# VectorE's share of the exponentials computed from two parts instead of three, with 232 units instead of 200

## The chip, the cores and the metric

The kernel runs on one core of a Trainium2 chip: TensorE (PE) multiplies matrices, ScalarE (ACT) evaluates functions, VectorE (DVE) does elementwise work, GpSimd (POOL) does little here but issue accumulating DMAs, and SyncE (SP) issues the other DMAs. Each engine works through its own instructions in order. TensorE writes its results to eight PSUM banks of 128 x 512 fp32, and ScalarE and VectorE read them there. The metric is the time of one execution on the device in microseconds; where several executions were timed, their median.

## The reference

Two attention branches read the same x (2048 x 640) and are mixed by a gate. The first is full softmax attention with 32 heads of 20 dimensions, the second looks at 8 keys with a step of 2 positions.

```python
qkv = (x @ wqkv).reshape(B, S, 3, H, Dh)             # H = 32, Dh = 20, S = 2048, D = 640
# branch A
scores = jnp.einsum("bhqd,bhkd->bhqk", q, k) * scale
p = _softmax(scores, axis=-1)
a = jnp.einsum("bhqk,bhkd->bhqd", p, v) ... @ wo
# branch B: keys at position s - 2*w, w = 0..7, own weights
logits = jnp.einsum("bhsd,bhswd->bhsw", q, kg) * scale   # masked below 0
b = jnp.einsum("bhsw,bhswd->bhsd", softmax(logits), vg) ... @ wo
g = sigmoid((x * gate_w).sum(-1, keepdims=True))
return g * a + (1 - g) * b
```

Branch A needs 32 x 2048 x 2048 exponentials. That is 134 million, or 1.05 million per partition.

## The kernel before

Branch A is cut into 32 groups: 4 blocks of 512 queries times 8 quads of 4 heads. A group has 64 units; a unit is one head, 128 keys and 512 queries, so 128 x 512 scores in one PSUM bank, and there are 2048 units. For each unit TensorE multiplies keys and queries (L1318), an exponential turns the scores into weights in SBUF, and TensorE multiplies these with the values into one PSUM bank for the group (L1425). The four heads of a quad use four strips of 32 rows or columns of TensorE, so up to four such matmuls run at the same time. A column of ones beside the values gives the softmax's sum, and the maximum over the keys enters the query projection as a bound (`KM`, L717), so no pass for the maximum is needed.

The exponential of most units is done by ScalarE (`mk_exp`, L1376), two or three banks in one instruction, in turn from banks 0 to 2 and from banks 3 and 4. Bank 5 is added as a third one where it is free. The other units go to VectorE, through bank 5 or 7. For them VectorE makes the exponential out of bits. The scores are scaled so that adding a constant and converting to int16 (L1584, one unit) gives the bit pattern of a bf16 number t: the integer part becomes the exponent E and the fraction the mantissa m, so t = E times m with m from 1 to 2. That is 2 to a power, with the curve between two powers replaced by a straight line. The rest mends the curve, two units at a time. `xw` takes the mantissa bits (L1614) and `xe` the exponent bits (L1618, with one low mantissa bit set, `XMU`); m is squared (L1622) and multiplied with t (L1625), which gives E times m cubed. TensorE then adds three parts for each unit: t with the values, `xe` with the values, and `xw` with the values scaled by `XCUB` = 0.168 (`vP`, made by GpSimd at L1391 for each change of the quad, 28 times, and kept in two buffers). The sum is E (1.008 + m + 0.168 m^3), and the constant `XKAP` in `XB` brings it to the scale of ScalarE's exponentials. A buffer of t (there are three) is free again when the third of its users has been issued.

The order of all instructions is fixed when the program is built. A planner (`_Sched`, the lanes and the loop at the end of `_build`) keeps a clock for each engine with written costs and places work step by step; one step is one exponential of ScalarE with the score matmuls ahead of it. Lanes hold the other work: key, query and value projections (`gen_k`, `gen_q`, `gen_v`), the normalisation of a group (`gen_norm`), the local branch (`gen_F` for its projections and score products, `gen_V` for its values, `gen_K` for its softmax and its products with the values), the output projection (`gen_fold`) and VectorE's units (`gen_xm` for the scores, `gen_xr` for the conversion, `gen_x` for the rest). Projections take one of banks 5 and 7, as VectorE's units do. The table `SEG` holds twenty settings of the planner for each stretch of 24 steps. Where TensorE has room and its share of work in the last microseconds is under the first of these, a spare matmul fills it (`spare`, L1946 to L1961); some of these add zeros to a bank that is in use, with the zero tile `zt` as weights and the identity as the moving side (L1951).

`gen_K` multiplies weights and values of the local branch in VectorE (L1149, L1159) into product buffers `tmps`, and accumulating DMAs from GpSimd's queue (L1161) add these into `accs`. For want of space these lie on other tensors: the first two accumulators are `accW`, whose second half also holds the key weights `WkP`; the second product buffer is block 0 of `xT`, and the other accumulators are block 1. So `gen_K` waits until all key projections, the query projections of block 0 and all value projections are done.

## Time and profile before

| | |
|---|---|
| median of 3 runs | 874.95 us (871.74 to 876.6) |
| profiled execution | 872.27 us, its span 870.5 us |
| TensorE busy | 788.9 us (91%) |
| VectorE busy | 746.8 us (86%) |
| ScalarE busy | 853.4 us (98%) |
| GpSimd busy | 127.4 us (15%) |
| TensorE's granted clock | 1.00 throughout |

A row of the group view names the line, the engine, the operation, what it writes and reads with shapes and the count, then the busy time, the mean duration of one in ns, and the idle time of the engine just ahead of these instructions with what ended it. Durations of neighbouring instructions overlap, so that the sum of single durations is more than the busy time. A row of the waits names who waited for whom, the total in us, how often, and the longest. A row of the table by stretches gives its length, the busy time of PE, PEld (weight loads), DVE, ACT and POOL with their instructions, the clock, and the DMA's share and rate.

### The profile page before, as it was taken

The page shows a single profiled execution, that of the slowest core. Times are in us where ns is not written, and L with a number is a line of the kernel's source. Part 1 is how long each engine was busy: PE and PEld are TensorE (multiplying, and loading weights), DVE is VectorE, ACT ScalarE, POOL GpSimd, SP SyncE. Part 2 cuts the span into 40 slices and gives each one's busy share as a digit, 9 for nine tenths or more (in the row PEclk, how much of TensorE's full clock was granted, in tenths as well). Part 3 has the DMA queues.
Part 4 walks back from the last instruction along what each step waited for, and adds up shares of the span by engine and source line. Part 5 has one row for each costly group of instructions (what it writes and reads, how often), then busy time and mean ns, then how long its engine had stood idle before and what let it go on. Part 6 is the DMA issues. An engine that isn't in the chain of part 4 may idle for free.

```text
span 870.5 us, 16946 instructions
## 1 busy us (share of the span) xinstructions
PE 788.9 (91%) x6951; PEld 250.6 (29%) x7039; DVE 746.8 (86%) x1322; ACT 853.4 (98%) x793; POOL 127.4 (15%) x131
## 2 busy tenths in 40 slices
PE   9989998999998999988998889988899998888997
PEld 6322332223223222222232223322222222222234
DVE  6587977888877878988998989999999989999985
ACT  6999999999999999999999999999999999999997
POOL 1100010000100112223132220332300001243000
PEclk9999999999999999999999999999999999999999
DMA  8222001010010135456557662485810014585001
GB/s 184 43 50 51 6 17 13 5 28 6 6 16 8 38 55 94 66 97 107 103 107 108 97 100 32 92 134 99 127 10 6 9 17 77 89 134 92 1 2 32
DMA packets 141313, 51.33 MB, mean 59 GB/s; under 512 B 120628, under 2 KB 128948, under 8 KB 141236
## 3 DMA queue, kind: packets, MB, share of 16 engines
q0 software_dynamic: 13824, 31.46, 21.3%
q1 hardware_dynamic: 126612, 18.59, 13.8%
q8 instruction: 56, 0.92, 0.4%
q10 hardware_dynamic: 800, 0.18, 0.1%
q14 instruction: 21, 0.17, 0.1%
HBM read 16.14 MB, written 2.62 MB: 22 GB/s over the span
## 4 chain that ended last, share of the span: by engine, by line
ACT 80%; DVE 10%; PE 5%; DMA 4%; issue 1%; POOL 0%; DVEq 0%
ACT ebuf L1376 79%; DMA xT<-xT 2%; DMA accW<-tmps 1%; PE ps L1318 1%; DVE xT L1159 1%; DVE xt L1584 1%; DVE prod L1019 1%; DVE tmps L1159 1%; PE ps L506 1%; PE ps L1204 1%; DVE xw L1625 1%; DVE xw L1622 1%; PE ps L1228 1%; PE ps L1425 1%; DVE xe L1618 1%
## 5 line engine op out<-in xcount | busy, mean ns | idle before, releaser
L1376 ACT ACTIVATE ebuf<-ps 128x1536 bf16<-128x1536 f32 (+1 forms) x767 | 839.8, 1396 | 3.7 <-PE ps L1318 3.3
L1318 PE MATMUL ps<-qT,kT 32*128 32x512 bf16 x1984 | 296.6, 384 | 59.8 <-ACT ebuf L1376 45.9
L1425 PE MATMUL ps<-ebuf,vA 128*21 128x512 bf16 (+2 forms) x1964 | 216.4, 369 | 1.0 <-DVE rg L764 0.7
L1584 DVE TENSOR_SCALAR xt<-ps 128x512 int16<-128x512 f32 x200 | 136.1, 685 | 45.3 <-PE ps L1318 43.1
L1318 PEld LDWEIGHTS ps<-qT,kT 32*128 32x128 bf16 x1984 | 72.7, 91 | 326.7 <-ACT ebuf L1376 279.5
L1391 POOL TENSOR_SCALAR vP<-vA 128x1344 bf16<-128x1344 bf16 x28 | 39.1, 1397 | 423.3 <-DVE vA L635 241.2
L1625 DVE TENSOR_TENSOR xw<-xt,xw 128x1024 bf16<-128x1024 bf16 x100 | 69.5, 695 | 1.6
L1622 DVE TENSOR_TENSOR xw<-xw 128x1024 f16<-128x1024 bf16 x100 | 68.4, 684 | 0.0
L1425 PEld LDWEIGHTS ps<-ebuf,vA 128*21 128x21 bf16 x1964 | 45.3, 90 | 60.7 <-issue 49.6
L1425 PE MATMUL ps<-xw,vP 128*21 128x512 bf16 (+2 forms) x212 | 58.1, 372 | 0.0
L506 PE MATMUL ps<-xT,WqkB 128*128 128x512 bf16 x175 | 53.7, 383 | 4.1 <-issue 2.5
L1425 PE MATMUL ps<-xe,vA 128*21 128x512 bf16 (+2 forms) x212 | 56.4, 373 | 0.0
L1614 DVE TENSOR_SCALAR xw<-xt 128x1024 uint16<-128x1024 uint16 x100 | 43.6, 436 | 13.5 <-PE ps L1425 12.8
L1019 DVE TENSOR_TENSOR prod<-qk 128x1024 bf16<-128x1024 bf16 x80 | 52.6, 688 | 0.2
L1161 POOL DMA_DIRECT2D accW<-tmps x36 | 32.2, 971 | 129.7 <-DVE tmps L1159 93.3
L1425 PE MATMUL ps<-xt,vA 128*21 128x512 bf16 (+2 forms) x212 | 48.7, 373 | 0.2 <-DVE rg L764 0.2
L506 PE MATMUL ps<-xT,WqP 128*128 128x512 bf16 x138 | 42.8, 383 | 2.2 <-issue 2.0
L1618 DVE TENSOR_SCALAR xe<-xt 128x1024 uint16<-128x1024 uint16 x100 | 44.5, 445 | 0.0
L506 PE MATMUL ps<-xT,accW 128*128 128x512 bf16 x125 | 38.3, 383 | 1.8 <-issue 1.1
L1951 PE MATMUL ps<-ident,zt 128*128 128x512 bf16 x106 | 34.9, 385 | 0.3 <-issue 0.3
L506 PE MATMUL ps<-WvA,oBacc 128*128 128x320 bf16 x160 | 31.2, 302 | 1.2 <-DVE qT L720 0.9
L720 DVE TENSOR_SCALAR qT<-ps 128x512 bf16<-128x512 f32 x32 | 22.0, 688 | 11.1 <-PE ps L717 5.3
(134 smaller groups left out, 801.2 us busy)
## 6 DMA issues: line engine op xcount, KB each, us to landing
accW<-tmps POOLq DMA_DIRECT2D x36, 320.0 KB, 4.2
accW<-xT POOLq DMA_DIRECT2D x24, 320.0 KB, 4.1
xT<-xT POOLq DMA_DIRECT2D x24, 320.0 KB, 4.2
WqkB<-in_B_wqkv_dram SPq DMA_DIRECT2D x40, 160.0 KB
xT<-tmps POOLq DMA_DIRECT2D x12, 320.0 KB, 4.6
WqP<-in_A_wqkv_dram SPq DMA_DIRECT2D x135, 20.0 KB
x_tm<-in_A_x_dram SPq DMA_DIRECT2D x8, 320.0 KB
out_dram<-outsb SPq DMA_DIRECT2D x24, 80.0 KB
```

The costliest lines, as they stand in the source:

```text
L506: ins = e.matmul(o, l, r, start=(k0 + k == 0), stop=(k0 + k == n - 1))
L1019: t = T("dve", lambda e, r=r, q_ap=q_ap, k_ap=k_ap: e.tensor_tensor(prod[r][:, :, :], q_ap, k_ap, ALU.mult), reads=["qB", "kB"], writes=[( ...
L1318: return e.matmul(o, kT[js, q, kb * P:(kb + 1) * P], qT[g % NQT][js, :], start=True, stop=True)
L1376: return T("act", lambda e: e.activation(ebuf[:, 512 * p:512 * (p + n)], ps[:, b0 * 512:(b0 + n) * 512], ACTF.Exp, scale=LN2 / ONE), reads ...
L1391: T("pool", lambda e, r=r, q=q: e.tensor_scalar(vP[r % NVP][:, :, :], vA[:, q, :, :], XCUB, 1.0, op0=ALU.mult, op1=ALU.mult), reads=[("vA" ...
L1425: ins = e.matmul(bank[OB][32 * j:32 * j + DH + 1, o:o + w], vv, ap[:, w * i:w * i + w], start=st and i == 0, stop=sp and i == len(ks) - 1)
L1584: r = T("dve", lambda e, b=b, i=i, sl=sl: e.tensor_scalar(xt[sl][:, 512 * i:512 * i + 512].bitcast(I16), bank[b], XB, 0.0, op0=ALU.add, op ...
L1614: T("dve", lambda e, r=r, t0=t0: e.tensor_scalar(xw[r][:, :].bitcast(U16), t0.bitcast(U16), 0x007F, 0x3F80, op0=ALU.bitwise_and, op1=ALU.b ...
L1618: tx = T("dve", lambda e, r=r, t0=t0: e.tensor_scalar(xe[r][:, :].bitcast(U16), t0.bitcast(U16), 0x7F80, XMU, op0=ALU.bitwise_and, op1=ALU ...
L1622: T("dve", lambda e, r=r: e.tensor_tensor(xw[r][:, :].bitcast(F16), xw[r][:, :], xw[r][:, :], ALU.mult), reads=[], writes=[("xw", r)], cos ...
L1625: t = T("dve", lambda e, r=r, t0=t0: e.tensor_tensor(xw[r][:, :], t0, xw[r][:, :].bitcast(F16), ALU.mult), reads=tk, writes=[("xw", r)], c ...
L1951: T("pe", lambda e: e.matmul(bank[OB], zt[:, :], ones4, start=False, stop=False, skip_group_check=True), reads=["ident", "zt"], accum=[("o ...
```

## The change

VectorE's units use two parts in place of three. The mantissa bits are now combined with the exponent of one half, so `xw` holds m/2, and one multiplication with t gives E times m^2 / 2; there is no square. TensorE adds `xe` with the values and `xw` with the values, so E (1.016 + m^2 / 2). The part with t itself, GpSimd's scaled values `vP` and the code that planned them go, and a buffer of t is free as soon as the product has been issued. `XKAP` and `XMU` have new values.

The number of VectorE's units comes out at 232 instead of 200, and most rows of `SEG` are new, so all work is placed anew. In the built programs ScalarE's exponentials are 306 of three units and 449 of two, where they were 314 and 453.

Space has moved too. The key weights `WkP` have a tile of their own. `zt` has two columns in place of 128; the first matmuls of the program, which used it, take 128 zeroed columns of `oTd`. The zero spares take the identity as weights and, as the moving side, the two columns of `zt` read 256 times (`zrow`). For the first block, `gen_K` no longer waits for the projections (`dead0`); until these are done it uses only the first product buffer.

```diff
-XKAP = 2.174928977877578
+XKAP = 1.512810100254
 XB = 127.0 * ONE - ONE * float(np.log2(XKAP))
-XMU = 0x0001
-XCUB = 0.16796875
+XMU = 0x0002
...
 SEG = {
-    0: (0.68, -1e9, 20, 20, 0, 8, 380000.0, 1, 500.0, 0, 0.6, 40, 20, 600.0, 14000.0, 3, 6, 4, -1, 30.0),
+    0: (0.68, 300.0, 34, 12, 60, 10, 360000.0, 0, 0.0, 0, 0.6, 60, 20, 3000.0, 14000.0, 3, 6, 4, -1, 30.0),
...
-    zt = sb([P, P], BF16, "zt")
+    zt = sb([P, 2], BF16, "zt")
+    zrow = fap(zt, zt[:, 0:1], [[0, 256], [1, 2]])
...
-    WkPt = accW[:, 2 * D:4 * D]
+    WkPt = sb([P, 2 * D], BF16, "WkP")
...
-    NVP = 2
-    vP = [sb([P, KBN, 4 * VW], BF16, "vP%d" % i) for i in range(NVP)]
...
+    T("dve", lambda e: e.memset(oTd[:, 0, 0:P], 0.0), writes=["zw"])
...
+    def dead0():
+        return bool(fdone.get(0) and vBdone.get(0)) and all(i in kl and kl[i].done and GI[(0, i)] in ql and ql[GI[(0, i)]].done
+                                                           for i in range(1, NQUAD)) and all(i in vl and vl[i].done for i in range(4))
+
     def gen_K(tc):
...
-        while not (all(i in kl and kl[i].done and GI[(0, i)] in ql and ql[GI[(0, i)]].done for i in range(1, NQUAD)) and all(i in vl and vl[i].done for i in range(4))):
+        while tc > 0 and not dead0():
             yield ("poll",)
...
-                m = tmctr[0] % NTM
+                m = tmctr[0] % NTM if tc > 0 or dead0() else 0
...
-    def vp_make(r):
-        q = GO[QL[r]][1]
-        vpdone.add(r)
-        T("pool", lambda e, r=r, q=q: e.tensor_scalar(vP[r % NVP][:, :, :], vA[:, q, :, :], XCUB, 1.0, op0=ALU.mult, op1=ALU.mult),
-          reads=[("vA", q, g) for g in range(6)], writes=[("vP", r % NVP)], cost=1600)
...
-                    vv = vA[:, q, kb, VW * j:VW * j + DH + 1] if part < 2 else vP[QW[min(g, HG)] % NVP][:, kb, VW * j:VW * j + DH + 1]
+                    vv = vA[:, q, kb, VW * j:VW * j + DH + 1]
...
-                xleft[ids[i]] = 3
-                xpend.append((("xt", sl, i), xt[sl][:, 512 * i:512 * i + 512], un, 0, g, r, ids[i], ("t", sl)))
+                xleft[ids[i]] = 2
...
-            T("dve", lambda e, r=r, t0=t0: e.tensor_scalar(xw[r][:, :].bitcast(U16), t0.bitcast(U16), 0x007F, 0x3F80, op0=ALU.bitwise_and, op1=ALU.bitwise_or),
-              reads=tk, writes=[("xw", r)], cost=XTS)
-            yield ("dve", XTS, 0.0)
             xbusy[r] = 4
             tx = T("dve", lambda e, r=r, t0=t0: e.tensor_scalar(xe[r][:, :].bitcast(U16), t0.bitcast(U16), 0x7F80, XMU, op0=ALU.bitwise_and,
                                                                 op1=ALU.bitwise_or),
                    reads=tk, writes=[("xe", r)], cost=XTS)
+            yield ("dve", XTS, 0.0)
+            T("dve", lambda e, r=r, t0=t0: e.tensor_scalar(xw[r][:, :].bitcast(U16), t0.bitcast(U16), 0x007F, 0x3F00, op0=ALU.bitwise_and,
+                                                           op1=ALU.bitwise_or),
+              reads=tk, writes=[("xw", r)], cost=XTS)
             yield ("dve", 690.0, 0.0)
-            T("dve", lambda e, r=r: e.tensor_tensor(xw[r][:, :].bitcast(F16), xw[r][:, :], xw[r][:, :], ALU.mult),
-              reads=[], writes=[("xw", r)], cost=690)
-            yield ("dve", 690.0, 0.0)
-            t = T("dve", lambda e, r=r, t0=t0: e.tensor_tensor(xw[r][:, :], t0, xw[r][:, :].bitcast(F16), ALU.mult),
+            t = T("dve", lambda e, r=r, t0=t0: e.tensor_tensor(xw[r][:, :], t0, xw[r][:, :], ALU.mult),
                   reads=tk, writes=[("xw", r)], cost=690)
             xcred[0] -= 1
-            xput_t(sl)
+            xfree.append(sl)
...
-            T("pe", lambda e: e.matmul(bank[OB], zt[:, :], ones4, start=False, stop=False, skip_group_check=True),
+            T("pe", lambda e: e.matmul(bank[OB], ident[:, :], zrow, start=False, stop=False, skip_group_check=True),
```

## The prediction

> **What bounds the kernel now.** I read the profile's page first: the engine totals and the 40 slices.

> ```profile
> span 870.5 us, 16946 instructions
> PE 788.9 (91%) x6951; PEld 250.6 (29%) x7039; DVE 746.8 (86%) x1322; ACT 853.4 (98%) x793; POOL 127.4 (15%) x131
> DVE  6587977888877878988998989999999989999985
> ACT  6999999999999999999999999999999999999997
> PEclk9999999999999999999999999999999999999999
> L1376 ACT ACTIVATE ebuf<-ps 128x1536 bf16<-128x1536 f32 (+1 forms) x767 | 839.8, 1396 | 3.7 <-PE ps L1318 3.3
> ```

> ScalarE is busy in 98% of the span, and 839.8 us of that is one line, the 767 exponentials of L1376. Before them it idled 3.7 us in all. VectorE is next, and full in the second half. Then the table by stretches, to see whether this holds everywhere, and the start and the end:

> ```profile
> core 0: us, PE busy (x) PEld busy (x) DVE busy (x) ACT busy (x) POOL busy (x), PEclk, DMA share, GB/s
> 120.00:150.00 30.00, 27.19 (x209) 7.53 (x210) 23.48 (x38) 29.19 (x28) 2.97 (x2) 1.00 0.13 21
> 450.00:480.00 30.00, 27.07 (x264) 8.79 (x264) 26.79 (x39) 29.57 (x29) 9.77 (x11) 1.00 0.71 115
> 600.00:630.00 30.00, 24.56 (x218) 6.76 (x220) 27.60 (x45) 29.57 (x28) 10.47 (x12) 1.00 0.88 145
> 750.00:780.00 30.00, 25.96 (x231) 7.09 (x231) 28.79 (x42) 30.00 (x28) 11.38 (x12) 1.00 0.70 115
> 780.00:810.00 30.00, 26.69 (x241) 7.24 (x241) 29.51 (x50) 30.00 (x28) 7.56 (x8) 1.00 0.49 87
> 18.64 12.75 ACT L1376 ACTIVATE ebuf<-ps 128x1536 bf16<-128x1536 f32 x11 [0.80 <-PE ps L1318]
> 866.82 0.44 ACT L923 ACTIVATE WvB<-ps 128x320 bf16<-128x320 f32 x1 [2.34 <-PE ps L865]
> ```

> Even where VectorE is fullest (29.51 of 30 us at 780 to 810) ScalarE has 30.00: VectorE's work runs beside the exponentials. The waits and the chain say who waits for whom:

> ```profile
> PEld ps L1318 <- ACT ebuf L1376: 279.5, 587, 1.0
> ACT ebuf L1376 <- PE ps L1318: 3.3, 9, 0.8
> ACT 80%; DVE 10%; PE 5%; DMA 4%; issue 1%; POOL 0%; DVEq 0%
> ```

> TensorE's score matmuls wait for ScalarE to free their banks 587 times, and the other way round only 9 times, 3.3 us. So a microsecond of exponentials taken from ScalarE is a microsecond of time, as long as scores still come early. The chain's 10% on VectorE are short pieces of the local branch and the query projections in the middle; there the slack is thin.

> **The change part by part.** Units are 128x512 blocks of scores; there are 2048. In the built programs ScalarE has 314 exponentials of three units and 453 of two before, 306 and 449 after: 1848 units become 1816, VectorE's 200 become 232.

> ```profile
> L1376 ACT ACTIVATE ebuf<-ps 128x1536 bf16<-128x1536 f32 x314 | 516.4, 1645 | 1.8 <-PE ps L1318 1.5
> L1376 ACT ACTIVATE ebuf<-ps 128x1024 bf16<-128x1024 f32 x453 | 510.2, 1223 | 1.9 <-PE ps L1318 1.8
> ```

> *ScalarE.* The two forms differ by 1645 - 1223 = 422 ns, one unit. Records overlap (516.4 + 510.2 is more than 839.8), so the fixed part is what is left of the busy time: (839.8 - 1848 x 0.422) / 767 = 0.078 us. Removed: 32 x 0.422 + 12 x 0.078 = **14.4 us**. This is the gain, all of it on the path.

> *VectorE.* Each pair of units loses its square, and there are 16 more pairs.

> ```profile
> L1584 DVE TENSOR_SCALAR xt<-ps 128x512 int16<-128x512 f32 x200 | 136.1, 685 | 45.3 <-PE ps L1318 43.1
> L1625 DVE TENSOR_TENSOR xw<-xt,xw 128x1024 bf16<-128x1024 bf16 x100 | 69.5, 695 | 1.6
> L1622 DVE TENSOR_TENSOR xw<-xw 128x1024 f16<-128x1024 bf16 x100 | 68.4, 684 | 0.0
> L1618 DVE TENSOR_SCALAR xe<-xt 128x1024 uint16<-128x1024 uint16 x100 | 44.5, 445 | 0.0
> L1614 DVE TENSOR_SCALAR xw<-xt 128x1024 uint16<-128x1024 uint16 x100 | 43.6, 436 | 13.5 <-PE ps L1425 12.8
> ```

> Removed 100 x 0.684 = 68.4 us; added 32 x 0.685 + 16 x (0.695 + 0.445 + 0.436) = 47.1 us; net -21.3 us. The product now takes two bf16 operands instead of bf16 and f16; I price it at the same 695 ns, since L1622, with two bf16 operands, is at 684. VectorE lies beside ScalarE, so this by itself is worth nothing: it pays for keeping up with a path that is 14.4 us shorter. It does not help evenly. Counted in the programs' order, VectorE has 71 units beside exponentials 553 to 744 before and 86 after: 15 x 0.685 + 7.5 x 1.576 = +22.1 us against 35.5 x 0.684 = -24.3 us. There VectorE's work falls by 2.2 us while ScalarE's falls by 15 x 0.422 = 6.3 us. VectorE was full there, so up to 4.1 us of the gain can be given back; ScalarE lost nothing at 29.51 of 30 us, so I take 1.5.

> *TensorE.* The parts per unit go from three to two:

> ```profile
> L1425 PE MATMUL ps<-ebuf,vA 128*21 128x512 bf16 x1792 | 209.0, 382 | 0.9 <-DVE rg L764 0.7
> L1425 PE MATMUL ps<-xw,vP 128*21 128x512 bf16 x192 | 56.5, 385 | 0.0
> L1951 PE MATMUL ps<-ident,zt 128*128 128x512 bf16 x106 | 34.9, 385 | 0.3 <-issue 0.3
> ```

> 2368 value matmuls of 512 columns (1792 + 3 x 192) become 1762 + 2 x 222 = 2206, at 209.0 / 1792 = 0.117 us some 19 us less. TensorE waits for ScalarE 279.5 us, so the cover is large and this is worth nothing. The spare matmuls with zeros (106 plus 3 before, 82 after) now have the identity as weights and a two-element row of zeros read 256 times as the moving side. No row shows such an operand; by L1951's shape I take the same duration, and keep the rest for a rival.

> *GpSimd.* The 28 scaled copies go:

> ```profile
> L1391 POOL TENSOR_SCALAR vP<-vA 128x1344 bf16<-128x1344 bf16 x28 | 39.1, 1397 | 423.3 <-DVE vA L635 241.2
> L1614 DVE TENSOR_SCALAR xw<-xt x100: 359/419/1532, 54.5 to 851.2; 128x1024 uint16<-128x1024 uint16 x100
> POOL vP L1391 <- PE ps L1425: 146.4, 11, 26.5
> accW<-tmps POOLq DMA_DIRECT2D x36, 320.0 KB, 4.2
> ```

> L1614's longest is 1532 ns against a median of 419, about one vP (1397) longer. Mean less median, over 100 of each, is (436 - 419) x 100 = 1.7 us, off the path. [...] The accumulating DMAs queued behind a waiting vP (up to 26.5 us) on GpSimd's queue also start freely; they land in 4.2 us as before.

> *Local branch sooner.* The first accumulating DMA stands behind the 276th exponential before and the 268th after; until the other buffer is free only one product buffer is used, so each product waits for the last one's landing (4.2 us). The counts of products, DMAs and queue entries are unchanged, SP's too. Nothing else waits on this branch until its fold, some 100 exponentials on; cost 0, and at best it lifts part of the 3.3 us that exponentials wait. Bounds -3.3 to +1.

> *Placement.* Of 32 query projections, those finished three exponentials or fewer ahead of their first score number five before and two after (the first of all in both). The last value group of head quads 6 and 7 now stands directly ahead of the value matmuls that need it; before it was two exponentials ahead. TensorE then waits for its evacuation, with the next scores behind it:

> ```profile
> L635 DVE CAST vA<-ps x23: 285/657/659, 20.0 to 287.7; 128x480 bf16<-128x480 f32 x19, 128x160 bf16<-128x160 f32 x4
> L712 DVE TENSOR_SCALAR qabs<-ps 128x512 uint16<-128x512 uint16 x32 | 21.9, 684 | 8.9 <-PE ps L506 8.8
> L720 DVE TENSOR_SCALAR qT<-ps 128x512 bf16<-128x512 f32 x32 | 22.0, 688 | 11.1 <-PE ps L717 5.3 <-PE ps L1318 4.5 <-PE ps L617 0.8
> L717 PE MATMUL ps<-qabs,KM x21: 379/389/390, 57.7 to 822.3; 128*128 128x512 bf16 x21
> ```

> That is 0.3 us for the short form (the shortest of L635), at most one queued VectorE operation of 0.7 us more: 0 to 1.0 us, I take 0.5.

> *Start and end.* One more memset, of the 128 zero columns, ahead of TensorE's first matmuls; these end before x arrives. The first score and the tail keep their instructions. Both 0.

> **The sum.** The profiled execution took 872.27 us (span 870.5 and 1.8 around it): 872.27 - 14.4 + 1.5 + 0.5 = **859.9 us**. The median of the runs, 874.95, lies 2.7 above that execution, the fastest run, 871.74, just below it; I state 860. The low end takes away all 3.3 us of waits as well and adds none: 872.27 - 14.4 - 3.3 = 854.6. The high end has the 4.1 us, the 1.0 us and two late queries of 0.684 + 0.389 + 0.688 = 1.76 us each, 866.5, and the 2.7 us of the median: 869.

> **The rivals.**

> *VectorE takes over as the bound.* For it: its slices are at 9 from the middle on, and the chain is already 10% there. If in those 10% a shorter exponential stream gains nothing, and the 4.1 us come on top, the gain is 14.4 x 0.9 - 4.1 = 8.9 us: 863. Against it: 30.00 of ScalarE beside 29.51 of VectorE. Still faster.

> *Late queries: slower.* Two score banks serve both VectorE's units and every projection, and 32 more units hold them. If query projections are pushed out until scores wait for the whole chain of 1.76 us, the point from which the gain is gone is 14.4 / 1.76 = 8 of the 32; all 32 would give 872.3 - 14.4 + 56 = 914. Against it: only two of 32 stand so close in the order, and the present five cost at most 0.8 us each.

> *The change does not give what the counts say, through slow zero rows.*

> ```profile
> 17.16 0.59 PE L1291 MATMUL ps<-xT,ident 128*128 128x512 bf16 x2
> ```

> Two such matmuls in a row take 0.59 us, one takes 0.385, so one streams in 0.205. If the repeated two-element row streams at half rate, 82 x 0.205 = 16.8 us if all stood in the way of scores: 877. It decides from 12.4 / 82 = 0.15 us each on the path. Against it: spares are placed where TensorE has nothing to do, with 279.5 us of waiting as cover.

> *The clock.* TensorE has some 19 us less work. If the granted clock fell to half in one stretch of 30 us, its 27 us of work would need 54: about 24 us, 884. Against it: the stretch at 600 had 24.56 us of TensorE work at 1.00. [...]

> **How the numbers follow.** About 0.5%, 4.4 us, is what a measurement here can tell from no change. Forecast 0.72; VectorE as the bound 0.14; late queries 0.06; zero rows 0.04; clock 0.02; several small waits that just eat the gain 0.02. Faster: 0.72 + 0.14, and 0.02 of the late queries, 0.88. Same: 0.01 of the late queries, 0.02 of the zero rows, the 0.02 of small waits, 0.05. Slower: the rest, 0.07. The range 854.6 to 869 holds the first two cases and leaves out some 0.15 with their own tails.

> **What would show it.** 755 exponentials at the same 1645 and 1223 ns, L1376's line near 825 us, idle before it below 8 us; VectorE near 725 us busy; GpSimd near 88 us; no vP rows; the clock at 1.00. It is wrong if exponentials wait for scores more than 10 us, if the zero spares last longer than 385 ns, or if ScalarE's share falls below 97%.

## The result and the profile after

The changed kernel takes 864.14 us in the median of 4 executions (862.73 to 867.12), the kernel before 874.52 (871.74 to 876.60). The ratio is 0.9888, with a 95% interval of 0.9847 to 0.9929: faster by 1.1%. The forecast was 860 us; the median lies 4 us above it, inside the range. The profiled execution of the changed kernel took 865.48 us.

The lines of its page that answer to those shown of before (engine totals, slices of VectorE and of the clock, the group of the exponentials, the shares of the chain):

```profile
span 863.7 us, 16606 instructions
PE 798.3 (92%) x6862; PEld 246.9 (29%) x6862; DVE 716.9 (83%) x1303; ACT 839.3 (97%) x781; POOL 87.3 (10%) x103
DVE  6586867878777779888888998998699898999885
PEclk9999999999999999999999999999699999999999
L1377 ACT ACTIVATE ebuf<-ps 128x1536 bf16<-128x1536 f32 (+1 forms) x755 | 826.3, 1412 | 11.3 <-PE ps L1319 11.3
ACT 84%; DMA 6%; PE 5%; DVE 3%; issue 1%; POOL 0%; SPq 0%; DVEq 0%
```

The exponentials' busy time went from 839.8 to 826.3 us, 13.5 us less, but the idle time ahead of them rose from 3.7 to 11.3 us, and one slice of the clock is no longer full. The span fell by 6.8 us: 13.5 less 7.6, and 0.9 elsewhere. So the work left ScalarE as forecast, and what has to be explained is 7.6 us of waiting, where the prediction's sum had set aside 2.0. Two of the prediction's own signs of being wrong came up: the exponentials waited more than 10 us, and the zero spares last 391 ns, more than the 385 it allowed.

The table by stretches shows where it is (us, busy time of each engine, then clock, DMA share and GB/s):

```profile
core 0: us, PE busy (x) PEld busy (x) DVE busy (x) ACT busy (x) POOL busy (x), PEclk, DMA share, GB/s
600.00:630.00 30.00, 26.59 (x183) 5.62 (x183) 23.39 (x41) 24.23 (x24) 3.82 (x5) 0.72 0.34 56
780.00:810.00 30.00, 27.88 (x214) 7.82 (x211) 27.61 (x49) 30.00 (x28) 5.19 (x6) 1.00 0.38 67
```

At 780 to 810 us, where VectorE was fullest before (29.51 of 30), it now has 27.61, and ScalarE still has 30.00. At 600 to 630 us ScalarE lost 5.77 of 30 us, and the granted clock is 0.72. The timeline of the changed kernel just ahead of that stretch tells how it begins (start, duration, instruction, and in brackets the idle time before it with what ended it):

```profile
598.87 0.39 PE L1411 MATMUL ps<-ebuf,vA 128*21 128x512 bf16 x3
599.23 0.39 PE L1319 MATMUL ps<-qT,kT 32*128 32x512 bf16 x2
599.30 1.49 DVE L1160 TENSOR_TENSOR tmps<-vB,attnT 128x1280 f32<-128x1280 bf16 x1 [2.08 <-DMA accW<-tmps]
600.71 0.68 DVE L1566 TENSOR_SCALAR xt<-ps 128x512 int16<-128x512 f32 x1
601.45 0.11 PEld L1319 LDWEIGHTS ps<-qT,kT 32*128 32x128 bf16 x4 [2.12 <-DVE xt L1566]
601.45 0.63 PE L1319 MATMUL ps<-qT,kT 32*128 32x512 bf16 x4 [1.83 <-ACT ebuf L1377]
602.13 1.45 ACT L1377 ACTIVATE ebuf<-ps 128x1536 bf16<-128x1536 f32 x1 [0.69 <-PE ps L1319]
```

Read it from the third row. A product of the local branch (L1160) waits 2.08 us on VectorE for an accumulating transfer to release its buffer. In VectorE's order the conversion that frees a score bank (L1566) stands behind it and starts only at 600.71, as the product ends. The next score matmul in TensorE's order needs that bank (the row of its weight load names L1566): TensorE stands still for 1.83 us. The exponential loses 0.69 us directly. More is lost after that, as three stretches around this place show, cut where the clock changes:

```profile
595.00:601.90 6.90, 5.04 (x39) 1.24 (x38) 4.82 (x8) 6.44 (x7) 1.75 (x3) 1.00 0.93 161
601.90:618.97 17.07, 17.07 (x78) 2.88 (x79) 11.14 (x23) 12.00 (x11) 1.69 (x2) 0.50 0.31 57
618.97:636.04 17.07, 14.86 (x145) 4.05 (x146) 16.32 (x25) 16.83 (x16) 3.47 (x4) 1.00 0.48 75
```

From 601.90 the clock is 0.50 for 17.07 us. TensorE is busy in all of these, and ScalarE in 12.00. This is the clock rival of the prediction, on a smaller scale. The exponentials' waits inside the two falls and directly behind them add up to some 6 of the 11.3 us. The other fall, 3.41 us from 410.7, follows a pause of 1.18 us that begins at 408.23; there `oBacc` (L1177) had waited 1.31 us for a transfer.

### The profile page after: what moved, and what is told of

Read it like the earlier page. It is cut to its first block, busy times and chain, and to the rows that moved or that the text cites. A ratio compares the mean times of both kernels' runs of the same rounds, so it can differ in the third digit from the quotient of the medians.

```text
span 863.7 us, 16606 instructions
## 1 busy us (share of the span) xinstructions
PE 798.3 (92%) x6862; PEld 246.9 (29%) x6862; DVE 716.9 (83%) x1303; ACT 839.3 (97%) x781; POOL 87.3 (10%) x103
## 4 chain that ended last, share of the span: by engine, by line
ACT 84%; DMA 6%; PE 5%; DVE 3%; issue 1%; POOL 0%; SPq 0%; DVEq 0%
ACT ebuf L1377 84%; DMA accW<-tmps 3%; DMA accW<-xT 2%; PE ps L1319 2%; PE ps L503 1%; PE ps L1411 1%; DVE tmps L1160 1%; DVE accW L1150 1%; PE ps L1229 1%; DMA x_tm<-in_A_x_dram 1%; PE ps L1205 0%; ACT L_sb L1093 0%; DVE xt L1566 0%; POOL accW L1162 0%; DVE attnT L1123 0%
## 5 line engine op out<-in xcount | busy, mean ns | idle before, releaser
L1377 ACT ACTIVATE ebuf<-ps 128x1536 bf16<-128x1536 f32 (+1 forms) x755 | 826.3, 1412 | 11.3 <-PE ps L1319 11.3
L1566 DVE TENSOR_SCALAR xt<-ps 128x512 int16<-128x512 f32 x232 | 157.5, 685 | 52.9 <-PE ps L1319 51.2
L1604 DVE TENSOR_TENSOR xw<-xt,xw 128x1024 bf16<-128x1024 bf16 x116 | 79.1, 682 | 1.6
L503 PE MATMUL ps<-xT,WqkB 128*128 128x512 bf16 x200 | 62.9, 390 | 1.4 <-DVE lgtr L1022 1.2
L1411 PE MATMUL ps<-xw,vA 128*21 128x512 bf16 (+2 forms) x250 | 64.1, 373 | 0.0
L1411 PEld LDWEIGHTS ps<-ebuf,vA 128*21 128x21 bf16 x1926 | 43.1, 90 | 64.0 <-issue 54.8
L1600 DVE TENSOR_SCALAR xw<-xt 128x1024 uint16<-128x1024 uint16 x116 | 48.7, 420 | 3.9 <-PE ps L1411 3.7
L503 PE MATMUL ps<-xT,WqP 128*128 128x512 bf16 x155 | 47.8, 391 | 0.3 <-DVE xt L1566 0.2
L503 PE MATMUL ps<-xT,WkP 128*128 128x512 bf16 x140 | 41.8, 384 | 0.0
L717 DVE TENSOR_SCALAR qT<-ps 128x512 bf16<-128x512 f32 x32 | 22.1, 690 | 16.7 <-PE ps L714 16.6
L503 PE MATMUL ps<-WvA,oBacc 128*128 128x320 bf16 x160 | 32.0, 307 | 1.2 <-DVE outsb L825 1.2
L979 DVE CAST qk<-ps 128x512 bf16<-128x512 f32 x40 | 27.2, 681 | 6.6 <-PE ps L503 6.3
L614 PE MATMUL ps<-WvA,xT 128*128 128x160 bf16 (+1 forms) x320 | 30.6, 234 | 0.0
L503 PE MATMUL ps<-woA_r,oTd 128*128 128x320 bf16 x144 | 29.5, 301 | 0.0
L503 PE MATMUL ps<-xT,WvB 128*128 128x512 bf16 x100 | 29.3, 383 | 0.0
```

Of the source, the lines that this page charges most:

```text
L503: ins = e.matmul(o, l, r, start=(k0 + k == 0), stop=(k0 + k == n - 1))
L614: ins = e.matmul(bank[b][:, i_ * wn:(i_ + 1) * wn], xT[:, kb // 4, c, (kb % 4) * P:(kb % 4 + 1) * P], WvA[:, c, w0:w0 + wn], start=(c == 0 ...
L979: give(b, T("dve", lambda e, dst=dst, b=b: e.tensor_copy(dst, bank[b]), reads=[("bk", b)], writes=[key], cost=690))
L1377: return T("act", lambda e: e.activation(ebuf[:, 512 * p:512 * (p + n)], ps[:, b0 * 512:(b0 + n) * 512], ACTF.Exp, scale=LN2 / ONE), reads ...
L1411: ins = e.matmul(bank[OB][32 * j:32 * j + DH + 1, o:o + w], vv, ap[:, w * i:w * i + w], start=st and i == 0, stop=sp and i == len(ks) - 1)
L1566: r = T("dve", lambda e, b=b, i=i, sl=sl: e.tensor_scalar(xt[sl][:, 512 * i:512 * i + 512].bitcast(I16), bank[b], XB, 0.0, op0=ALU.add, op ...
```

## The experiments

The theory: the exponentials shrank as forecast; VectorE waits for accumulating transfers, and the conversions behind in its order wait with it; TensorE pauses for want of a score bank; the clock falls and stays low. The rivals: the zero spares in their new form are slow; VectorE's relief is worth nothing, or VectorE is the bound; the gain comes from the new settings and not from the arithmetic.

### Two pauses filled with zero matmuls

```diff
+    FILL = {354: 5, 527: 8}
+
+    def fill_z(n):
+        if n and cnt[0] + xcnt_[0] > 0:
+            for _ in range(n):
+                T("pe", lambda e: e.matmul(bank[OB], ident[:, :], zrow, ...), ..., cost=0.0)
...
         mk_qk(s, xu)
+        fill_z(FILL.get(s, 0))
```

> The changed kernel with 13 more zero matmuls, 5 ahead of the unit matmul that waits at 408.2 us and 8 ahead of the one that waits at 599.6 us; every other instruction in the same order. Clock theory (TensorE's pauses of 1.2 and 1.8 us let the granted clock fall to 0.50 for 3.4 and 17.1 us, and exponentials then wait): the clock stays at 1.00 up to the tail, idle before the exponentials falls from 11.3 to about 4.5 us, profiled time about 859, ratio to the kernel before about 0.983. Rival (the late accumulating DMAs and the waits behind them cost the time by themselves, the clock only goes with them): 863 to 866 as without the fill, idle about 11 us.

Measured: 858.42 us (857.84 to 859.49, 5 executions), ratio 0.9818 [0.9798, 0.9838]. The timeline at the same place, the chief row of the exponentials' waits, and the same three stretches, moved by the 2.14 us by which this execution is earlier:

```profile
597.16 1.49 DVE L1160 TENSOR_TENSOR tmps<-vB,attnT 128x1280 f32<-128x1280 bf16 x1 [2.13 <-DMA accW<-tmps]
597.36 1.91 PE L1993 MATMUL ps<-zt,ident 128*128 128x512 bf16 x8
599.31 0.60 PE L1319 MATMUL ps<-qT,kT 32*128 32x512 bf16 x4
599.96 1.45 ACT L1377 ACTIVATE ebuf<-ps 128x1536 bf16<-128x1536 f32 x1 [0.71 <-PE ps L1319]
...
ACT ebuf L1377 <- PE ps L1319: 4.7, 8, 0.9
...
592.86:599.76 6.90, 6.83 (x47) 1.94 (x46) 4.77 (x8) 6.39 (x7) 1.79 (x3) 1.00 0.92 159
599.76:616.83 17.07, 15.51 (x140) 4.21 (x142) 15.40 (x31) 16.26 (x16) 1.64 (x2) 0.90 0.41 63
616.83:633.90 17.07, 16.14 (x121) 4.00 (x117) 17.06 (x29) 17.01 (x16) 5.67 (x6) 1.00 0.59 107
```

VectorE's wait is the same (2.13 us), and so is the direct loss (0.71 us). Only the pause is gone, filled by eight zero matmuls, and with it the long fall: ScalarE has 16.26 of 17.07 us in place of 12.00. The waits of the exponentials fall from 11.3 to 4.7 us. So at this place the clock behind the pause, not VectorE's wait itself, cost most of the lost time. The next run, on the same chip and with the pause left open (1.55 us), has the long fall and takes 862.04 and 864.95 us. One thing did not come as expected: the clock was not at 1.00 up to the tail. The 0.90 above is a fall of 3.41 us from 613.26, behind a pause of 0.89 us.

### The zero spares in their old form

```diff
-    zt = sb([P, 2], BF16, "zt")
-    zrow = fap(zt, zt[:, 0:1], [[0, 256], [1, 2]])
+    zt = sb([P, P], BF16, "zt")
...
-            T("pe", lambda e: e.matmul(bank[OB], ident[:, :], zrow, ...
+            T("pe", lambda e: e.matmul(bank[OB], zt[:, :], ones4, ...
```

> The changed kernel with the zero spares as before: 128 zero columns as weights, the identity as the moving side; same order. If rows of zeros as the moving side keep TensorE less active (rival for the clock's fall), the clock stays at 1.00 and the time is near 859. If only the pauses count, the clock falls as in the changed kernel (mean near 0.987), 863 to 866; the zero spares last 385 to 391 ns either way.

Measured: 862.04 and 864.95 us, ratio 0.9874 [0.9836, 0.9911], no different from the changed kernel. The group of the spares and the clock's slices of this run, then the group of the spares in the changed kernel:

```profile
L1918 PE MATMUL ps<-ident,zt 128*128 128x512 bf16 x82 | 27.4, 388 | 0.0
PEclk9999999999999999999999999999699999999999
```

```profile
L1919 PE MATMUL ps<-zt,ident 128*128 128x512 bf16 x82 | 27.7, 391 | 0.0
```

388 against 391 ns. In the run before, eight repeated rows back to back took 1.91 us, of which each further one adds (1.91 - 0.38) / 7 = 0.22 us; three plain rows of L503, at 567.92 of the same run, took 0.82 us, (0.82 - 0.39) / 2 = 0.22 us. So the repeated two-element row streamed as fast as a plain one. The long fall of the clock is there with either form (17.07 us, here from 601.3). The rival of the slow zero rows is out.

### The arithmetic with the settings of before

```diff
 SEG = {
-    0: (0.68, 300.0, 34, 12, 60, 10, 360000.0, 0, 0.0, 0, 0.6, 60, 20, 3000.0, 14000.0, 3, 6, 4, -1, 30.0),
+    0: (0.68, -1e9, 20, 20, 0, 8, 380000.0, 1, 500.0, 0, 0.6, 40, 20, 600.0, 14000.0, 3, 6, 4, -1, 30.0),
...
```

> The changed kernel with the old table of planner settings: two parts, but VectorE's units come out at 216. If the count of units sets the gain, ScalarE has 16 units x 0.422 = 6.8 us more exponentials than the changed kernel and 7.2 us fewer than the kernel before: 865 without falls of the clock, ratio 0.991. If the arithmetic alone gave the gain, 860. If the settings that fit the old work don't fit the new, more than 870 with idle before the exponentials over 12 us.

Measured: 868.76 us (864.91 to 872.99, 8 executions), ratio 0.9934 [0.9910, 0.9958]. With the settings of before the planner places 216 units, and the exponentials take 832.5 us:

```profile
L1378 ACT ACTIVATE ebuf<-ps 128x1536 bf16<-128x1536 f32 (+1 forms) x765 | 832.5, 1418 | 8.0 <-PE ps L1320 5.3
```

16 units more on ScalarE than in the changed kernel are 16 x 0.422 = 6.8 us by the prediction's price; the line is 6.2 us longer. The time is 3.8 us above the 865 expected without falls; the profiled execution has a fall of 6.83 us at 400.4. With the settings of before, the two-part arithmetic (and the new places in memory, which this run keeps) gives 0.7% of the 1.1%, a good half of the gain; the intervals are too wide to say it more closely. The rest needs the new settings.

### A square that nobody reads

```diff
+    xs_ = sb([P, 1024], BF16, "xs")
...
+            t_sq = T("dve", lambda e, r=r: e.tensor_tensor(xs_[:, :], xw[r][:, :], xw[r][:, :], ALU.mult),
+              reads=[("xw", r)], writes=["xs"], cost=0.0)
```

The planner does not see these 116 instructions, so the placement stays, but for the end of VectorE's order, and VectorE carries its old kind of load.

> The changed kernel with a square of 1024 columns put back for each of the 116 pairs, written to a buffer that nobody reads; the order of the rest is kept but for the last 45 instructions of VectorE. VectorE gets 116 x 0.684 = 79 us more work, 796 us of 864. If VectorE's work lies beside the exponentials, the time moves by less than 5 us. If VectorE is nearly the bound (rival: it was the square's removal that paid for the units), exponentials wait for more than 25 us and the time is over 880.

Measured: 886.00 us (881.58 to 891.64, 4 executions), ratio 1.0153 [1.0101, 1.0204]: slower than the kernel before. Engine totals, shares of the chain, and the exponentials' waits of the profiled execution, which took 881.58 us:

```profile
PE 800.3 (91%) x6865; PEld 250.1 (28%) x6865; DVE 787.7 (90%) x1419; ACT 844.2 (96%) x781; POOL 87.4 (10%) x103
ACT 49%; DVE 32%; PE 11%; DMA 5%; issue 2%; POOL 0%; SPq 0%; DVEq 0%
ACT ebuf L1378 <- PE ps L1320: 18.6, 37, 1.4
```

VectorE's share of the chain goes from 3% to 32%, and exponentials wait 37 times in place of 19. The time is the rival's, over 880; the idle time before the exponentials, 22.8 us, stays short of its 25. The clock is part of the median: the two longest executions had 0.969 and 0.972. The profiled one, with 0.991 no lower than the changed kernel, still took 16 us more. In this order the 232 units can't be carried with the square: VectorE's relief is what makes the shorter stream of exponentials possible.

### The arithmetic alone undone

```diff
-XKAP = 1.512810100254
+XKAP = 2.174928977877578
...
+            T("dve", lambda e, r=r: e.tensor_tensor(xw[r][:, :].bitcast(F16), xw[r][:, :], xw[r][:, :], ALU.mult),
+              reads=[], writes=[("xw", r)], cost=690)
...
+                vv = vA[...] if part < 2 else vP[QW[min(g, HG)] % NVP][...]
```

> The changed kernel with the arithmetic alone undone: the square on VectorE, the third value matmul and GpSimd's scaled values are back, the settings of the changed kernel are kept, and the planner, which now reckons 0.69 us more of VectorE for two units, places 188 units in the place of 232. Theory of the prediction (the change pays by what the relieved VectorE can take from ScalarE): 44 units x 0.422 = 18.6 us more of exponentials than the changed kernel's 826.3, 845; with 4 to 11 us of idle time, 876 to 884. Rival (the settings carry the gain, not the arithmetic): as the changed kernel, 862 to 868.

Measured: 887.03 us (884.95 to 888.96, 4 executions), ratio 1.0139 [1.0108, 1.0170].

```profile
L1380 ACT ACTIVATE ebuf<-ps 128x1024 bf16<-128x1024 f32 (+1 forms) x779 | 847.4, 1353 | 13.1 <-PE ps L1322 9.9 <-PE ps L1325 2.8
PE 815.1 (92%) x7016; PEld 252.3 (28%) x7016; DVE 726.4 (82%) x1287; ACT 860.3 (97%) x805; POOL 128.7 (15%) x131
```

The exponentials take 847.4 us, 21.1 more than in the changed kernel, where 18.6 were expected. The expectation left out that there are 24 instructions more, 1.9 us at the prediction's 0.078. The time is 3 us above the range given, with 13.1 us of idle time in place of 4 to 11. The settings do not carry the gain by themselves: without the arithmetic the planner places only 188 units, and the kernel is slower than before. They were made for the two-part arithmetic, though; what the best settings for three parts would give was not tried, beyond those of the kernel before.

### Eight pauses filled

```diff
-    FILL = {354: 5, 527: 8}
+    FILL = {47: 4, 277: 5, 354: 5, 527: 8, 541: 4, 585: 4, 617: 4, 743: 4}
```

> The changed kernel with zero matmuls put at the two pauses already filled and at six more, where the run with two filled still left TensorE without work for 0.8 to 1.05 us (at 70, 322, 612, 661, 696 and 836 us). 24 more zero matmuls, each about 0.2 us, after the queries' scores and ahead of the task that waits; nothing else moved. Theory (a pause lets the clock fall): the falls that the run with two filled had, 3.41 us at 613.3 and 3.41 us at 848.8, go; the exponentials' idle time goes from 4.9 to some 4 us, the time to 857 to 858 and the spread between executions narrows. Rival (the clock falls for another reason, the fill at two places was luck): falls stay or come elsewhere, 858 to 864. Against both: if the zero matmuls themselves delay the scores behind them, the exponentials' idle time grows, 860 and over.

Measured: 862.30 us (860.64 to 863.98, 4 executions), ratio 0.9850 [0.9820, 0.9880]. This is the rival's number and not the theory's: the six pauses are gone and the fall at 613.3 too (the one near the end stays, now at 853.7), but the clock now falls for 3.41 us at 570.4 and for 6.83 us at 751.3, and the exponentials wait 9.1 us. That the new zero matmuls stand in the way of the scores, the third possibility above, does not account for it: behind the one at 322 us an exponential waits 1.01 us, where it was 0.90, and behind the other five the timeline shows no wait. Stretches of 3.41 us, the length of the shortest falls, placed so that the falls begin at their edges. The two falls begin 180.89 us apart, 53 times 3.413; that the edges run on at this step to places without a fall is my assumption:

```profile
566.99:570.40 3.41, 1.38 (x43) 0.58 (x37) 2.73 (x4) 2.81 (x3) 1.46 (x2) 1.00 0.84 162
382.69:386.10 3.41, 2.50 (x20) 0.61 (x18) 1.20 (x3) 3.41 (x4) 0.00 (x0) 1.00 0.55 96
386.10:389.51 3.41, 2.39 (x49) 0.92 (x49) 2.88 (x7) 1.91 (x3) 0.00 (x0) 1.00 0.03 7
747.88:751.29 3.41, 2.37 (x21) 0.49 (x21) 3.04 (x7) 3.41 (x4) 0.94 (x2) 1.00 0.93 164
751.29:758.10 6.81, 6.81 (x68) 1.69 (x66) 5.16 (x8) 6.26 (x6) 2.60 (x3) 0.50 0.90 158
```

A new pause of 1.83 us at 567.99, behind a 2.21 us wait of VectorE for a transfer, lies whole in one such stretch (TensorE 1.38 of 3.41) and the clock falls. Another of 1.79 us at 385.19 is cut by the edge at 386.10, so that both stretches keep 2.4 to 2.5 us of work, and it does not fall. But the stretch ahead of the fall at 751.29 has no pause above 0.41 us and 2.37 us of work. So a fall may follow a pause that lies within one stretch, but also a stretch without one.

How little TensorE works in such a stretch does not decide alone either. The first row is the stretch ahead of the long fall in the changed kernel. The other two are of the run with the settings of before, cut at the edges of its own fall and whole stretches further on:

```profile
598.49:601.90 3.41, 1.58 (x16) 0.32 (x13) 2.60 (x3) 2.95 (x3) 0.97 (x3) 1.00 0.85 152
397.01:400.42 3.41, 2.52 (x21) 0.65 (x21) 3.26 (x7) 3.41 (x4) 0.86 (x1) 1.00 0.91 144
468.68:472.09 3.41, 1.77 (x41) 0.92 (x42) 1.38 (x2) 1.72 (x2) 0.00 (x0) 1.00 0.47 25
```

With 1.58 and with 2.52 us of work the clock falls behind the stretch, with 1.77 it does not. Which transfer lands late differs from run to run, and so do the edges: counted from the start of the span, the fall at 601.90 in the changed kernel begins some 1.2 us past a whole number of 3.413 us, the one at 570.40 here some 0.4 us. Filling the pauses of one trace does not fill those of the next.

### The same 13 zero matmuls where there is no pause, and the two fills once more

```diff
-    FILL = {354: 5, 527: 8}
+    FILL = {334: 5, 507: 8}
```

> The changed kernel with the same 13 zero matmuls as the run with two pauses filled, but put 20 steps earlier, where TensorE makes no long pause. Theory (what helped was that the pauses are gone, not that there are more zero matmuls): the pauses at about 408 and 600 us stay, and with them a fall of the clock of 10 us or more and some 10 us of idle time before the exponentials; 862 to 867, as the changed kernel. Rival (any 13 zero matmuls do): 857 to 860 with a clock of 0.995 or more.

> The run with two pauses filled once more, on the chip of the other two kernels of this call. It tells whether the 862.3 with eight pauses filled against the 858.4 with two came from the six more (the chip was another one). If the two fills carry it: 857.5 to 860, clock 0.995 or more. If it was the chip or the luck of the transfers: 860 to 864, with falls of the clock in the middle of the run.

Measured, on one chip: moved, 861.64 us (859.26 to 862.01, 4 executions), ratio 0.9857 [0.9834, 0.9879]; the two fills again, 858.79 us (857.44 to 860.37, 4 executions), ratio 0.9825 [0.9801, 0.9849]. The two fills repeat their time on another chip, with a clock of 0.993 to 0.999, so their 858.4 was not luck; but they too have a fall in the middle in the profiled execution (6.83 us at 747.2), and the intervals of two and eight fills overlap. The moved ones lie between the two ranges I gave, just below that of the theory, and one half of what I expected of them failed: the pause at 408 us and its fall (3.41 us at 411.4) stayed, the one at 600 us did not, and a fall of 6.83 us came at 749.3. The timeline of the moved fills shows what they met:

```profile
577.92 1.91 PE L1993 MATMUL ps<-zt,ident 128*128 128x512 bf16 x8
580.63 1.94 ACT L1377 ACTIVATE ebuf<-ps 128x1024 bf16<-128x1024 f32 x2 [1.25 <-PE ps L1319]
...
599.38 1.49 DVE L1160 TENSOR_TENSOR tmps<-vB,attnT 128x1280 f32<-128x1280 bf16 x1 [1.09 <-DMA accW<-tmps]
601.53 0.60 PE L1319 MATMUL ps<-qT,kT 32*128 32x512 bf16 x4 [0.86 <-DVE xt L1566]
```

Where TensorE has no pause, the eight zero matmuls stand in the way of the scores: the next exponential waits 1.25 us, where it had waited for nothing. Further on, VectorE's wait is 1.09 us in place of 2.08, and the pause 0.86 us; that the delay ahead of them caused this is likely, but not shown. The five moved ones, at 383.5 us, met a pause after all: in the changed kernel one of 1.22 us begins at 384.92, and here it is gone. So the control is not clean. The intervals overlap between the moved fills and the fills at the pauses. What speaks for the mechanism is the timelines at 599 us (an open pause of 1.83 us with the long fall, a filled or a short one without), not the medians.

### A later landing time in the plan

```diff
-    DLAT, DSLACK = 4700.0, 500.0
+    DLAT, DSLACK = 6500.0, 500.0
```

> The changed kernel planned anew with the planner's landing time of an accumulating transfer at 6.5 us in the place of 4.7: it sets the instruction that waits for the transfer later in VectorE's order. It places 224 units in the place of 232, 8 more on ScalarE: 8 x 0.422 = 3.4 us more of exponentials. Theory (the pauses of TensorE come from VectorE waiting in order for these transfers): VectorE's waits for accumulating transfers become fewer than the 8.2 us over tmps, TensorE's pauses shorter than 1.8 us, no long fall of the clock, exponentials' idle time 4 to 7 us; time 858 to 864. Rival (VectorE's waits have nothing to do with the pauses): pauses and the idle time of 11 us stay, 864 + 3.4 = 867 to 869.

Measured at 6.5 us: 864.88 us (864.44 to 865.93, 4 executions), ratio 0.9888 [0.9864, 0.9912]. The shares of its chain and the chief row of the exponentials' waits:

```profile
ACT 93%; PE 5%; DVE 1%; issue 0%; DVEq 0%
ACT ebuf L1377 <- PE ps L1319: 7.1, 6, 4.5
```

The transfers' 6% of the chain are gone, VectorE no longer waits for any accumulating transfer, the longest pause of TensorE is 0.96 us, and the clock stayed at 0.997 to 0.999 in all four executions (0.981 to 0.989 in the changed kernel's). So the pauses above 1 us went with VectorE's waits, as the theory has it. It is no proof, since all work was placed anew. The time did not gain: it is just above the 858 to 864 of the theory. 8 units went back to ScalarE (829.3 us of exponentials), and the exponentials' idle time is 8.4 us, more than half of it one wait of 4.5 us that came with the new placement, where TensorE does 24 matmuls of L503 for the output between two scores.

At 7.0 us the same happened on a larger scale:

> The changed kernel planned anew with the landing time of an accumulating transfer at 7.0 us (4.7 before): 228 units in the place of 232, 4 x 0.422 = 1.7 us more of exponentials than 826.3. At 6.5 us the clock stayed at 0.997 to 0.999 in four executions. Theory (VectorE's waits for these transfers make the pauses): no wait over tmps among VectorE's longest, clock 0.996 or more in all executions, idle time before the exponentials 3 to 8 us, 857 to 864. Rival (the run at 6.5 us was spared by its order alone): falls in the middle of the run, clock 0.99, 864 and over.

Measured: 871.57 us (869.97 to 873.98, 10 executions), ratio 0.9981 [0.9968, 0.9995]. The stretch with its longest wait:

```profile
467.00:481.50 14.50, 10.27 (x49) 2.63 (x48) 6.94 (x12) 2.92 (x4) 0.00 (x0) 0.65 0.39 60
ACT ebuf L1377 <- PE ps L1319: 16.4, 7, 10.3
```

VectorE has no wait for an accumulating transfer here either. Yet TensorE has a pause of 1.26 us (at 541.72, behind a product of the local branch that waited for nothing), the clock falls for 10.24 us from 471.3, and one exponential waits 10.3 us. TensorE's timeline inside that stretch shows what stands ahead of its scores:

```profile
468.69 0.31 PE L503 MATMUL ps<-WvA,oBacc 128*128 128x320 bf16 x1 [0.96 <-DVE outsb L825]
...
473.22 1.91 PE L503 MATMUL ps<-xT,WqP 128*128 128x512 bf16 x4 [0.89 <-DVE lgtr L1022]
475.92 0.61 PE L714 MATMUL ps<-qabs,KM 128*128 128x512 bf16 x1 [0.79 <-DVE qabs L709]
477.41 1.01 PE L1319 MATMUL ps<-qT,kT 32*128 32x512 bf16 x5 [0.88 <-DVE qT L717]
```

A whole query projection, at half the clock, stands between the last score and the next one, after a run of output projections: the prediction's rival of the late queries, which the changed kernel itself doesn't have. My expectation that without the transfers' waits the clock would stay up was wrong: here it falls behind other short pauses, the longest of 0.96 us.

## Why the prediction was right, and where its sum was off

- **ScalarE, 14.4 us on the path.** Right. The page shows 755 exponentials, 826.3 us against 839.8, 13.5 us less; with the pauses filled it is 825.2, 14.6 less. The price of a unit, 422 ns as the difference of the two forms, also held in the run with 216 units (6.2 us measured, 6.8 by the price). The single forms themselves lasted longer than before, 1665 and 1240 ns.
- **VectorE, "by itself worth nothing", 1.5 us given back where it is full.** The busy time came out at 716.9 us, 8 below the forecast of 725, since its operations on units became shorter, too: 418, 420 and 682 ns against 445, 436 and 695. The longest of L1600 is 543 ns, where its like (L1614) had 1532 in the kernel before, at 687.89, while a scaled copy ran on GpSimd from 687.80 to 689.14. In the three-part run, with GpSimd's copies back, two of the three are long again, the mantissa bits (L1618) and the product (L1629): 438 and 723 ns, and 1003 and 1790 at the longest. Nothing was given back where VectorE was full: 30.00 us of ScalarE at 780 to 810. The phrase needs its second half: the unread square cost 22 us in the median (16 in the profiled execution), so the relief is the condition of the gain. The rival that VectorE takes over as the bound came true only there.
- **The value group of head quads 6 and 7, 0.5 us.** Right: TensorE waits 0.42 us for this evacuation (L632) at 285.68, and an exponential 0.46 us at 286.65, where there was no wait before.
- **Zero spares at the same duration.** Right, 391 against 385 ns; the old form in the changed kernel lasts 388. The sign of being wrong, longer than 385 ns, was drawn too tight for such differences.
- **GpSimd and TensorE, no effect.** 87.3 us as forecast. The 19 us less of TensorE can't be read from the totals, 798.3 after and 788.9 before. In the trace of before 88 matmuls have no record (6951 against 7039 weight loads), in that of after none are missing. How much this can be, two executions of the kernel with two fills show: 796.6 us with all 6875 records, 781.2 with 6788. And 20.5 us of the 798.3 ran at half speed. That TensorE's work had no effect is true of its amount; its pauses had one, by the clock.
- **Local branch opened sooner, cost 0.** With the old wait put back alone, the planner writes the very same order of instructions, so this edit by itself moves nothing. The waits of VectorE for the branch's transfers come with the placement: the longest over `tmps` went from 1.1 to 2.3 us. What in the placement did that was not taken apart, so the first cause of the pauses stays open.
- **Late queries.** Not in the changed kernel: its exponentials wait 19 times and at most 0.9 us. The plan with 7.0 us shows what the rival would have cost.
- **The clock, the step that failed.** I gave it 2 chances in 100 and priced it at 884, a whole stretch of 30 us at half the clock. No profile here shows such a stretch. Stretches of 30 us were too coarse to look for it: the 3.41 us ahead of the fall at 601.90 hold 1.58 us of TensorE work. It came on a small scale, 20.5 us at half speed in the middle of the profiled execution, and with two pauses filled the exponentials' idle time went from 11.3 to 4.9 us. There the profiled execution took 858.99 us, within a microsecond of the sum of 859.9. Part of the step was to take the clock of 1.00 in one execution of the kernel before for that of the kernel: its other executions had 0.991 to 1.000.
- **The sum.** It set 2.0 us aside for new waits (1.5 for VectorE, 0.5 for the value group), and 7.6 came. That makes the 5.6 us by which the profiled execution, 865.48, lies above 859.9; the other two differences, 0.9 less taken from ScalarE and 0.9 gained elsewhere, cancel. That the time stayed inside the range is in part luck: the room above 860 was made for VectorE, for late queries and for the median, and the clock used it.

## What to carry to other kernels

When a change takes work off the bounding engine, look at the engine that feeds it in stretches of a few microseconds, and not only at its total: a pause of 1.83 us cost 0.7 us by itself and some 4 more by the clock behind it. Follow the wait back to its first cause; here it was a transfer that held VectorE up for 2.08 us, with an unrelated conversion behind it in the program's order. A few zero matmuls in such a pause were cheap (eight of them in 1.91 us, and the direct wait of the exponential 0.71 us against 0.69), but only where the pause really is: in the way of scores the same eight cost 1.25 us.
